# Later loads, a transposed table of probabilities, and a state update moved behind its result, in a gated recurrence followed by an expert layer

## The chip, the cores and the metric

The kernel runs on one core of a Trainium2 chip. The metric is the device time of one execution in microseconds; of several runs, the median is given. A profile is one further execution, taken by the hardware profiler; its durations are used for sums, and its own time stands beside them.

Engines are named as in the profile: PE (TensorE, matmul), PEld (its weight loads), DVE (VectorE), ACT (ScalarE), POOL (GpSimd), SP (SyncE, which here only issues DMAs). A name with a q behind it (SPq) is the engine's instruction queue.

## The reference

Two blocks follow each other. The first is a gated linear recurrence over 768 positions, for 4 batches and 8 heads of 48 numbers:

```python
for t in range(S):
    state = alpha[:, :, t, :, None] * state + np.einsum('bhd,bhe->bhde', k[:, :, t], v[:, :, t])
    y[:, :, t] = np.einsum('bhd,bhde->bhe', q[:, :, t], state)
```

Its result, as rows x of 384 numbers (3072 rows), goes through four experts, weighted by probabilities:

```python
p = domain_probs / (domain_probs.sum(-1, keepdims=True) + 1e-09)
for e in range(E):
    h = np.maximum(x @ w1[e], 0.0)
    out += p[:, e:e + 1] * (h @ w2[e])
```

All inputs and the output are float32.

## The kernel before

**Units and groups.** The recurrence is cut into 24 units of 128 positions of one batch (all 8 heads), numbered 0 to 23 in the order block of positions, then batch. Units come in groups: group 0 has units 0 and 1, groups 1 to 5 have four units each, group 6 has units 22 and 23. For each group and each expert the kernel runs `up` (x @ w1, L710) for eight slices of the 1024 hidden columns, then `down` (h @ w2, L773). From group 1 on, both are computed from operands split into a top part and a rest in float32r, three products each: L745 is the `up` matmul (128x512, nine per slice), L814 the `down` matmul (128x384).

**Order.** The program's order on every engine is the order in which Python emits it. The attention of a unit is a generator with 17 steps (0 to 16, L432 to L703). `deal()` (L860) gives every step of units 2 to 23 a due time from assumed costs of `up` and `down`; `advance()` (L908) runs the steps that are due between two matmuls of `down` or two slices of `up`. Steps of one unit thus lie among the expert matmuls of an earlier group and among steps of the next unit. Units 11 to 17 tie two due times to the unit ahead (`TOGETHER`): their step 7 falls together with step 15 of the unit ahead, their step 11 with its step 16.

**One unit, late kind.** Units 10 to 19 are called `moved` in the code (L611). Step 0 turns the gates on DVE (L444) and lets SP load the next unit's gates into the same buffer (`sa`). Steps 1 and 2 do so for keys (`sk`, `rk`) and queries (`sq`, `rq`, and L170, L171). Steps 3 to 10 build scaled keys and queries. Step 11 computes the far and last near scores on PE (L602, L536) and turns the scaled keys on DVE (L614). Step 12 stores these turned keys to a DRAM buffer `over` (L623), step 13 loads them back into AT in another arrangement, in four DMAs (L630). Step 14 does nothing for these units. Step 15, `result()`, has 56 matmuls into `yps` (L652), copied to xT. Step 16 has 32 small matmuls of AT and the values rv into `sps` (L683), two multiply-and-add pairs on DVE that bring the state `st` up to date (L699, L700), and the load of the values of unit u + 2 into the same buffer rv (L702, issued at L165). Other units compute `sps` at L689 from an AT that PE has turned.

**The start.** Unit 0 has its own code, `first_unit` (L249), written out by hand, with steps of unit 1 in between (`next(other)`). It scores into two tiles, `diag` and `later_half`, which lie in the float32r weight buffers of later use. `take(li)` copies masked scores into `diag` by DVE; for level 0 these are the odd columns. On SP the order is: inputs of units 0 and 1; four pieces of w1 of expert 0 (`raw`, L202, 384 KB each); from L368 the inputs of unit 2 (14 DMAs, behind three POOL memsets); the probabilities (L944, 24 x 128 rows of 16 bytes); four pieces of w2 (L206); then the rest. After `first_unit` a hand-written list (L947) places the remaining steps of units 0 and 1 among the first `up` and `down`. `norm_probs` (L233) divides the probabilities by their sums, in four DVE operations after half of the first `up`.

**Weights.** SP loads raw weights once; ACT and DVE split them, POOL stores the split pieces to DRAM (`kept`), and SP loads them again for each later group (L195, 768 KB a piece). A load into a weight buffer waits for the matmuls that read the piece before it. SP issues in order, so a DMA that waits holds all behind it.

**Places.** Pools lie one behind the other in each partition: `const`, `wts` (w1, w2), `work` (first `dot`, 64 bytes, then raw, AT, QT, KT, xT), `hid` (`room`, 96 bytes that nothing uses, then hT and acc).

Of the kernel before, what the change touches and what calls it, by code (L numbers as in the profile page):

```python
# [10 lines left out]
F32 = mybir.dt.float32  # L11
# [5 lines left out]
AX = mybir.AxisListType  # L17
# [3 lines left out]
def kernel(  # L21
# [11 lines left out]
    nc = tc.nc  # L33

    B, H, S, D = q.shape
    E, DM, F = moe_w1.shape
    P = 128
    NCB = S // P
    NP = H // 2
    HD = 64  # L40
    QUAD = 32
    VD = D + QUAD
    KC = DM // P
    FCH = F // P
    NT = B * P
    NQ = 4
# [7 lines left out]
    n = np.arange(QUAD)[None, :]  # L54
# [8 lines left out]
    const = ctx.enter_context(tc.tile_pool(name="const", bufs=1))  # L63
    wts = ctx.enter_context(tc.tile_pool(name="wts", bufs=2))
    dram = ctx.enter_context(tc.tile_pool(name="dram", bufs=1, space=bass.MemoryType.DRAM))
    work = ctx.enter_context(tc.tile_pool(name="work", bufs=2))
# [4 lines left out]
    ident = ident_all[:, :P]  # L71
# [2 lines left out]
    NBLK = B * NCB  # L74
    p_all = const.tile([P, NBLK, E], F32, name="p_all")
    tot = const.tile([P, NBLK], F32, name="tot")

    near = const.tile([P, H, HALF], F32, name="near")
    lat = const.tile([P, H, P], F32, name="lat")
# [21 lines left out]
    rows_of = {nm: const.tile([P, n, H, D], F32, name=f"r{nm}") for nm, n in (("k", 1), ("q", 2), ("a", 1))}  # L101
    early = {nm: runs_of[nm].rearrange("p a n -> p (a n)")[:, :H * HD].rearrange("p (h d) -> p h d", d=HD)
             for nm in "akq"}
    work.tile([P, 2, H], F32, name="dot", bufs=1)
    hid.tile([P, 24], F32, name="room", bufs=1)
    spare = hid.tile([P, 4, NT], F32, name="hT", bufs=NQ)
    apart = {nm: spare[:, i].rearrange("p (h d) -> p h d", d=HD) for i, nm in enumerate("akq")}
    values = [const.tile([P, H, VD], F32, name=f"rv{i}") for i in range(2)]
# [34 lines left out]
    fresh = lambda gi: gi == 1  # L143


    def load(u, names):
        if u >= len(units):
            return
        cb, b = units[u]
        for nm in names:  # L150
            src = srcs[nm][b, :, cb * P:(cb + 1) * P, :].rearrange("h s d -> s h d")
            if u == by_pairs and nm == "q":
                nc.gpsimd.memset(rows_of["a"], 1.0)
            if u == in_runs and nm != "v":
                nc.gpsimd.memset(runs_of[nm][:, :, RUN - HD // 4:], 0.0)
            for g in range(P // QUAD if u >= in_runs and nm != "v" else 0):
                i, tail = divmod(g, 2)
                off, n = (QUAD, RUN - HD // 4) if tail else (0, RUN)
                runs = srcs[nm][b].rearrange("(a i) s d -> i a (s d)", i=2)[
                    i, :, cb * P * D:(cb + 1) * P * D].rearrange("a (t n) -> t a n", t=QUAD)  # L160
                nc.sync.dma_start(out=runs_of[nm][QUAD * g:QUAD * (g + 1), :, :n],
                                  in_=runs[:, :, off:off + n])
            if u >= in_runs and nm == "a":
                continue
            nc.sync.dma_start(out=raw(u, nm)[:, :, :D], in_=src)  # L165
            if u >= by_pairs and nm == "q":
                odd = srcs["q"][b].rearrange("h (t two) d -> two t h d", two=2)[1, cb * HALF:(cb + 1) * HALF]
                decay = srcs["a"][b].rearrange("h (t two) d -> two t h d", two=2)[1, cb * HALF:(cb + 1) * HALF]
                for first in range(2):
                    nc.sync.dma_start(out=rows_of["q"][first::2, 1], in_=odd)  # L170
                nc.sync.dma_start(out=rows_of["a"][::2, 0], in_=decay)  # L171
# [13 lines left out]
    SPLIT_AT = {1: 2, 4: 3}  # L185
    BESIDE = [{1: 0, 2: 1, 3: 2, 4: 3}, {1: 2, 2: 3}]

    def load_piece(l, i, beside=False):
        if i >= E * NQ * LAST:
            return  # L190
        gi, k = divmod(i, E * NQ)
        e, c = divmod(k, NQ)
        if gi > l:
            w = wt[l][i] = parts_of(l)
            nc.sync.dma_start(out=w.bitcast(F32), in_=kept[l][k])  # L195
            return
        if l == 1 and gi == 0 and not beside:
            return
        w = work.tile([P, KC * QF], F32, name="raw", bufs=RAW)
        wt[l][i] = w  # L200
        if l == 0:
            nc.sync.dma_start(  # L202
                out=w.rearrange("p (c f) -> p c f", f=QF),
                in_=moe_w1[e].rearrange("(c p) f -> p c f", p=P)[:, :, c * QF:(c + 1) * QF])
        else:
            nc.sync.dma_start(  # L206
                out=w.rearrange("p (c d) -> p c d", d=DM),
                in_=moe_w2[e].rearrange("(c p) d -> p c d", p=P)[:, c * FPQ:(c + 1) * FPQ])
# [22 lines left out]
            next(splitting[-1])  # L231

    def norm_probs():  # L233
        nc.vector.reduce_sum(out=tot, in_=p_all, axis=AX.X)
        nc.vector.tensor_scalar_add(out=tot, in0=tot, scalar1=1e-9)
        nc.vector.reciprocal(out=tot, in_=tot)
        nc.vector.tensor_mul(p_all, p_all, tot.unsqueeze(2).broadcast_to([P, NBLK, E]))


    def halves(t, m):  # L240
# [8 lines left out]
    def first_unit(fill, other):  # L249
# [29 lines left out]
        def same_q(li):  # L279
            old, new = (used(t, li) for t in QTs[li:li + 2])  # L280
            nc.scalar.copy(out=new[:, :, :, 0, :], in_=old[:, :, :, 0, :])
# [30 lines left out]
        def take(li, outs):  # L312
            for i in range(2):
                to = diag[:, NP * i:NP * (i + 1)]
                if li < 0:
                    nc.vector.copy_predicated(
                        to, masks_all[:, 6 * QUAD:].unsqueeze(1).broadcast_to([P, NP, HALF]), outs[i])
                    continue
                m = LEVELS[li]
                mk = masks[:, li, :].rearrange("p (b r) -> p b r", r=m)  # L320
                nc.vector.copy_predicated(
                    to.rearrange("p a (b two r) -> p a b two r", two=2, r=m)[:, :, :, 1, :],
                    mk.unsqueeze(1).broadcast_to([P, NP, QUAD // m, m]),
                    outs[i].rearrange("p a (b r) -> p a b r", r=m))
# [40 lines left out]
        same_q(4)  # L365
        next_k(3)
        same_k(3)
        load(2, "akq")  # L368
        products(3, part(second, QUAD))
        take(0, part(first, 0))  # L370
        same_q(5)
        next_q(5)
        scored(part(second, HALF, HALF), KTs[0], lambda p, i, s: plain[rows[i], p, keys[s]])
# [22 lines left out]
        for half, copy in ((0, nc.vector.tensor_copy), (1, nc.scalar.copy)):  # L396
            of = slice(NP * half, NP * (half + 1))
            copy(out=later_half[HALF:, of], in_=diag[HALF:, of])
        fill(1)
        next(other)  # L400

# [30 lines left out]
    def attention(u):  # L432
# [26 lines left out]
            turn("k", KT)  # L459
        else:  # L460
            nc.scalar.copy(out=KT, in_=turned(pair(rk)))
        dot = work.tile([P, 2, H], F32, name="dot", bufs=1)

        def pair_terms():
            both = rows_of["q"]
# [203 lines left out]
                nc.scalar.copy(out=AT, in_=turned(lambda p: KT[:, p, :]))  # L669


        for step in (turn_keys, result) if u >= half else (result, turn_keys):
            step()
            yield

        if cb < NCB - 1:
            KB = AT
            apart_ = u + 1 in in_pairs or moved
            sps = ps.tile([P, NP, 1 if apart_ else 2, D], F32, name="sps", tag="w")
            for p in range(NP if moved else 0):  # L680
                for g in range(P // QUAD):
                    at = QUAD * (NP * g + p)
                    nc.tensor.matmul(sps[QUAD * g:QUAD * (g + 1), p, 0],  # L683
                                     lhsT=KB.rearrange("x a n -> x (a n)")[:, at:at + QUAD],
                                     rhs=rv[:, 2 * p + g // 2, :D], start=True, stop=True)
            for p in range(0 if moved else NP):
                for i in range(2) if apart_ else [slice(0, 2)]:
                    rows = slice(HD * i, HD * (i + 1)) if apart_ else slice(0, P)
                    nc.tensor.matmul(  # L689
                        sps[rows, p], lhsT=KB[:, p, rows],  # L690
                        rhs=rv[:, 2 * p + i, :D] if apart_ else rv[:, 2 * p:2 * p + 2, :D],
                        start=True, stop=True)
            for i in range(2):
                rows = slice(HD * i, HD * (i + 1))
                old, add = st[rows, :, i, :], sps[rows, :, 0 if apart_ else i, :]
                if cb == 0:
                    nc.vector.tensor_copy(out=old, in_=add)
                else:
                    nc.vector.tensor_mul(old, old, decs[-1][rows].broadcast_to([HD, NP, D]))  # L699
                    nc.vector.tensor_add(old, old, add)  # L700
# [213 lines left out]
    with tc.manual_schedule():  # L914
# [11 lines left out]

        load(0, "aqkv")
        load(1, "akqv")
        for i in range(NQ):
            load_piece(0, i)  # L930


# [4 lines left out]
        def fill(times, n=P):  # L937
            for _ in range(times):
                nc.tensor.matmul(idle[:, :n], lhsT=zeros[:, :P], rhs=zeros[:, :n], start=True, stop=True)
# [1 line left out]
        runs = [None, attention(1)]  # L941
        fill(7)
        runs[0] = first_unit(fill, runs[1])
        nc.sync.dma_start(out=p_all, in_=moe_domain_probs.rearrange("(n p) e -> p n e", p=P))  # L944

        span = cost(0, 0, 0) * FCH / 2 + cost(1, 0, 0)
        waiting.extend((span * (k + 1) / 15, u, runs[u])  # L947
                       for k, u in enumerate([1, 1, 1, 0, 1, 0, *[1] * 8]))
        for fc in range(FCH):
            up(0, 0, fc, slice(0, 1))  # L950
            if fc == FCH // 2:
                norm_probs()
            advance(cost(0, 0, 0) / 2)
        down(0, 0, [0])
        while waiting:
# [44 lines left out]
```

## Time and profile before

| what | us |
|---|---|
| median of 3 runs | 1001.29 (999.69 to 1004.07) |
| the profiled execution | 1002.28 |
| its span, first to last instruction | 1000.5 |
| PE busy / DVE busy / ACT busy / POOL busy | 976.8 / 580.6 / 402.5 / 51.4 |
| L814 matmuls on `w`, x2112 | 380.7 |
| L745 matmuls on `w`, x1440 | 336.4 |
| DVE's L700 idle for `sps` of L683 | 22.0 in 9 |

Busy time of PE is that of matmuls in flight, whose ends are modelled. The mean granted clock of PE is 0.996 of full speed; it stands at 0.5 in two stretches of 3.41 us, from 16.62 and from 122.43 us, and at full speed from 6.38 us on otherwise, up to the last microsecond. In the chain that ended last, L814 has 38% of the span and L745 33%. DMA moved 210 MB, a mean of 210 GB/s.

A row of the timeline gives start, duration, engine, line, operation, out<-in, shapes and count, and in brackets how long the engine was idle before it and what ended that. A row of the waits gives who waited for whom: us in total, times, longest.

### The profile page before, as it was taken

How to read it: one execution, taken by the hardware profiler on the slowest of the kernel's cores; microseconds unless marked ns; L12 is line 12 of the kernel's file. 1: busy time of each engine (PE TensorE's matmuls, PEld its weight loads, DVE VectorE, ACT ScalarE, POOL GpSimd, SP SyncE). 2: the span in 40 equal slices, each digit the busy share in tenths (PEclk: the TensorE clock that was granted, in tenths of full speed). 3: DMA queues.
4: the chain of work that ended last, by engine and by line, in shares of the span. 5: the costliest groups of instructions: out<-in, count | busy, mean ns of one | idle time of the engine just before them, and what ended most of it. 6: DMA issues, size and time to landing. Idle time of an engine off the chain costs nothing.

```text
span 1000.5 us, 20763 instructions
## 1 busy us (share of the span) xinstructions
PE 976.8 (98%) x8388; PEld 866.4 (87%) x8388; DVE 580.6 (58%) x1198; ACT 402.5 (40%) x876; POOL 51.4 (5%) x94
## 2 busy tenths in 40 slices
PE   8899899999999999999999999999999999999998
PEld 7777677988989889889899899898898999999997
DVE  4788868476776656666755746766576521222222
ACT  4767655464452542523533413445334422111111
POOL 2000001000101000000000000000000000000000
PEclk9999999999999999999999999999999999999999
DMA  9898979685966885967967769868767406060511
GB/s 191 258 293 220 307 242 351 201 267 170 331 197 204 271 263 147 289 201 216 266 209 243 234 213 264 263 168 283 246 180 246 158 1 221 32 224 30 224 44 32
DMA packets 189999, 210.21 MB, mean 210 GB/s; under 512 B 111408, under 2 KB 165040, under 8 KB 189904
## 3 DMA queue, kind: packets, MB, share of 16 engines
q1 hardware_dynamic: 183440, 179.04, 59.0%
q0 software_dynamic: 6016, 29.49, 7.6%
q8 instruction: 66, 1.08, 0.4%
q10 hardware_dynamic: 448, 0.36, 0.1%
q14 instruction: 29, 0.24, 0.1%
HBM read 176.34 MB, written 32.51 MB: 209 GB/s over the span
## 4 chain that ended last, share of the span: by engine, by line
PE 83%; DVE 7%; ACT 5%; issue 2%; DMA 1%; SPq 1%; DVEq 0%; POOL 0%; ACTq 0%; POOLq 0%
PE ops L814 38%; PE one L745 33%; PE sc L536 4%; PE yps L652 3%; ACT qb L508 2%; PE far L602 1%; DVE near L546 1%; DVE w L220 1%; PE one L739 1%; DVE QT L515 1%; DVE hT L770 1%; PE tp L246 1%; DVE KT L529 1%; ACT KT L528 1%; DVE QT L444 1%
## 5 line engine op out<-in xcount | busy, mean ns | idle before, releaser
L814 PE MATMUL ops<-w,hT 128*128 128x384 f32 x2112 | 380.7, 338 | 1.0 <-DVE hT L770 1.0
L814 PEld LDWEIGHTS ops<-w,hT 128*128 128x128 f32 x2112 | 364.2, 188 | 6.1 <-DVE hT L770 2.5
L745 PE MATMUL one<-xT,w 128*128 128x512 f32 x1440 | 336.4, 393 | 0.0
L745 PEld LDWEIGHTS one<-xT,w 128*128 128x128 f32 x1440 | 269.3, 188 | 58.3 <-DVE hT L770 0.5
L747 ACT ACTIVATE hT<-one 128x512 fp32r<-128x512 f32 (+1 forms) x192 | 108.0, 563 | 310.2 <-PE one L745 308.5
L770 DVE SCALAR_TENSOR_TENSOR hT<-one,hT 128x512 fp32r<-128x512 f32 (+1 forms) x192 | 121.6, 642 | 106.7 <-ACT hT L747 106.6
L508 ACT COPY qb<-QT 64x256 f32<-64x256 f32 x294 | 119.7, 407 | 77.6 <-DVE QT L515 62.2
L515 DVE TENSOR_TENSOR QT<-QT,AT 128x256 f32<-128x256 f32 x158 | 68.2, 431 | 79.9 <-ACT qb L508 78.6
L840 DVE SCALAR_TENSOR_TENSOR acc<-ops,p_all,acc 128x384 f32<-128x384 f32 x66 | 38.1, 612 | 89.1 <-PE ops L814 89.1
L546 DVE COPY_PREDICATED near<-masks,sc 128x256 f32<-128x256 uint8 x124 | 63.5, 512 | 16.3 <-PE sc L536 14.2
L536 PEld LDWEIGHTS sc<-qb,KT 128*64 128x64 f32 x1984 | 63.3, 138 | 9.7 <-issue 4.4
L536 PE MATMUL sc<-qb,KT 128*64 128x64 f32 x1984 | 67.9, 223 | 3.6 <-ACT qb L508 3.6
L529 DVE TENSOR_TENSOR KT<-KT,AT 128x256 f32<-128x256 f32 x161 | 68.0, 423 | 0.8 <-PE tp L246 0.8
L528 ACT COPY KT<-KT 128x256 f32<-128x256 f32 x124 | 51.5, 415 | 5.0 <-DVE KT L529 2.1
L739 PE MATMUL one<-xT,raw 128*128 128x256 f32 (+1 forms) x240 | 45.1, 340 | 0.4 <-ACT xT L416 0.4
L814 PE MATMUL ops<-raw,hT 128*128 128x384 f32 x128 | 44.7, 493 | 0.0
L517 DVE TENSOR_TENSOR AT<-AT 128x256 f32<-128x256 f32 (+1 forms) x138 | 41.5, 301 | 4.7
L458 ACT ACTIVATE AT<-AT,ident 128x512 f32<-128x512 f32 x22 | 15.9, 724 | 66.5 <-PE ops L814 45.2
L739 PEld LDWEIGHTS one<-xT,raw 128*128 128x128 f32 x240 | 38.1, 191 | 5.2 <-ACT xT L416 0.6
L652 PE MATMUL yps<-lat,rv 128*32 128x128 f32 x736 | 34.4, 279 | 2.6 <-ACT lat L627 2.6
L814 PEld LDWEIGHTS ops<-raw,hT 128*128 128x128 f32 x128 | 23.2, 190 | 13.9 <-issue 0.8
L745 PE MATMUL one<-raw,w 128*128 128x256 f32 x288 | 34.6, 279 | 0.0
(118 smaller groups left out, 630.7 us busy)
## 6 DMA issues: line engine op xcount, KB each, us to landing
w<-kept SPq DMA_DIRECT2D x144, 768.0 KB, 6.6
kept<-w POOLq DMA_DIRECT2D x32, 768.0 KB, 7.1
raw<-in_moe_w_dram SPq DMA_DIRECT2D x48, 384.0 KB, 7.3
rv<-in_v_dram SPq DMA_DIRECT2D x24, 192.0 KB, 3.2
rk<-in_k_dram SPq DMA_DIRECT2D x22, 192.0 KB, 3.4
rq<-in_q_dram SPq DMA_DIRECT2D x22, 192.0 KB, 7.2
out_dram<-acc POOLq DMA_DIRECT2D x22, 192.0 KB, 3.1
sa<-in_alpha_dram SPq DMA_DIRECT2D x44, 88.0 KB, 2.3
```

The lines of the kernel that those rows point to most:

```text
L508: nc.scalar.copy(out=qb[rows, :, i, :].rearrange("p a (b r) -> p a b r", r=m), in_=qv[rows])
L515: nc.vector.tensor_mul(qv, qv, spread(dv[:, :, :, 0], m))
L528: nc.scalar.copy(out=new[:, :, :, 1, :], in_=old[:, :, :, 1, :])
L529: nc.vector.tensor_mul(new[:, :, :, 0, :], old[:, :, :, 0, :], spread(halved(decs[li])[:, :, :, 1], m))
L536: nc.tensor.matmul(out[HALF * s:HALF * (s + 1), 2 * p:2 * p + 2, :], lhsT=KTs[li][:, p, HALF * s:HALF * (s + 1)], rhs=qbs[li][:, p, :, QUA ...
L546: nc.vector.copy_predicated(near.rearrange("p a (b two r) -> p a b two r", two=2, r=m)[:, :, :, 1, :], mk.unsqueeze(1).broadcast_to([P, H, ...
L652: nc.tensor.matmul(yps[QUAD * j:QUAD * (j + 1), c, :], lhsT=lhsT, rhs=rhs, start=begins, stop=ends)
L739: nc.tensor.matmul(one, lhsT=w[:, kc], rhs=xTs[gi][:, 0, kc, lo:hi], start=(kc == 0), stop=(kc == KC - 1))
L745: nc.tensor.matmul(one, lhsT=w[:, of_w, kc], rhs=x_part(gi, of_x)[:, kc, :n], start=k == 0, stop=k == len(turns) - 1)
L747: nc.scalar.activation(out=parts[0], in_=one, func=ACT.Relu)
L770: nc.vector.scalar_tensor_tensor(out=low, in0=x, scalar=0.0, in1=top.bitcast(F32), op0=ALU.max, op1=ALU.subtract)
L814: nc.tensor.matmul(sums[slot], lhsT=h, rhs=w, start=(n == begins[slot]), stop=(n == ends[slot]))
```

## The change

There are five edits.

1. Of the four first pieces of `raw`, the main program asks for two. The other two are asked for in `first_unit`, after take(0); a POOL copy of one column of `diag` into the first of them stands ahead of its DMA.
2. The inputs of unit 2 (`load(2, "akq")`) are asked for at the end of the work on `later_half`, behind a POOL copy of one column of it into `room`.
3. The probabilities are loaded as 24 rows of 128 x 4 numbers (`p_rows`, new, 2048 bytes in `const`), turned by four PE transposes into PSUM, and normalized from there. `norm_probs` becomes a generator that runs in the list of steps, at place 9.5. In the same list the second remaining step of unit 0 (its `sps` at L425, state copy and load of values) goes from place 5 to 10.5.
4. `dot` moves from the pool `work` to `hid`, ahead of `room`. With that, raw, AT, QT, KT and xT lie 64 bytes lower against w1 and w2, and hT lies against w1 and w2 as before.
5. The `sps` matmuls become a function `key_values()`. For the moved units it is called right behind `result()`, in step 15; for the others it stays in step 16. The DVE update and the load of values stay in step 16.

```diff
+    p_rows = const.tile([NBLK, P, E], F32, name="p_rows")
...
-    work.tile([P, 2, H], F32, name="dot", bufs=1)
-    hid.tile([P, 24], F32, name="room", bufs=1)
+    hid.tile([P, 2, H], F32, name="dot", bufs=1)
+    room = hid.tile([P, 24], F32, name="room", bufs=1)
...
-    def load(u, names):
+    def load(u, names, behind=None):
...
+        if behind is not None:
+            nc.gpsimd.tensor_copy(out=room[:, :1], in_=behind)
...
-    def load_piece(l, i, beside=False):
+    def load_piece(l, i, beside=False, behind=None):
...
         wt[l][i] = w
+        if behind is not None:
+            nc.gpsimd.tensor_copy(out=w[:, :1], in_=behind)
...
     def norm_probs():
-        nc.vector.reduce_sum(out=tot, in_=p_all, axis=AX.X)
+        tp = ps.tile([P, E, NBLK], F32, name="tp", tag="w")
+        for e in range(E):
+            nc.tensor.transpose(tp[:, e, :], p_rows[:, :, e], ident[:NBLK, :NBLK])
+        probs = tp.rearrange("p e n -> p n e")
+        nc.vector.reduce_sum(out=tot, in_=probs, axis=AX.X)
         nc.vector.tensor_scalar_add(out=tot, in0=tot, scalar1=1e-9)
         nc.vector.reciprocal(out=tot, in_=tot)
-        nc.vector.tensor_mul(p_all, p_all, tot.unsqueeze(2).broadcast_to([P, NBLK, E]))
+        nc.vector.tensor_mul(p_all, probs, tot.unsqueeze(2).broadcast_to([P, NBLK, E]))
+        yield
...
-        load(2, "akq")
         products(3, part(second, QUAD))
         take(0, part(first, 0))
+        for i in range(NQ // 2, NQ):
+            load_piece(0, i, behind=diag[:, 0, :1] if i == NQ // 2 else None)
...
             copy(out=later_half[HALF:, of], in_=diag[HALF:, of])
+        load(2, "akq", behind=later_half[:, 0, :1])
         fill(1)
...
-        for step in (turn_keys, result) if u >= half else (result, turn_keys):
-            step()
-            yield
-
-        if cb < NCB - 1:
-            KB = AT
+        def key_values():
             apart_ = u + 1 in in_pairs or moved
             sps = ps.tile([P, NP, 1 if apart_ else 2, D], F32, name="sps", tag="w")
...
+            return sps, apart_
+
+        for step in (turn_keys, result) if u >= half else (result, turn_keys):
+            step()
+            if step is result and moved:
+                new = key_values()
+            yield
+
+        if cb < NCB - 1:
+            sps, apart_ = new if moved else key_values()
...
-        for i in range(NQ):
+        for i in range(NQ // 2):
             load_piece(0, i)
...
-        nc.sync.dma_start(out=p_all, in_=moe_domain_probs.rearrange("(n p) e -> p n e", p=P))
+        nc.sync.dma_start(out=p_rows, in_=moe_domain_probs.rearrange("(n p) e -> n p e", p=P))
...
-        waiting.extend((span * (k + 1) / 15, u, runs[u])
-                       for k, u in enumerate([1, 1, 1, 0, 1, 0, *[1] * 8]))
+        runs.append(norm_probs())
+        waiting.extend((span * (k + 1) / 15, u, runs[u]) for k, u in (
+            *((k, 1) for k in range(3)), (3, 0), (4, 1), *((k, 1) for k in range(6, 10)),
+            (9.5, 2), (10, 1), (10.5, 0), *((k, 1) for k in range(11, 14))))
         for fc in range(FCH):
             up(0, 0, fc, slice(0, 1))
-            if fc == FCH // 2:
-                norm_probs()
             advance(cost(0, 0, 0) / 2)
```

More of the change, by code (lines that the diff above doesn't have):

```diff
@@ L461, in attention @@
             nc.scalar.copy(out=KT, in_=turned(pair(rk)))
-        dot = work.tile([P, 2, H], F32, name="dot", bufs=1)
+        dot = hid.tile([P, 2, H], F32, name="dot", bufs=1)
         def pair_terms():
@@ L683, in attention @@
                     nc.tensor.matmul(sps[QUAD * g:QUAD * (g + 1), p, 0],
-                                     lhsT=KB.rearrange("x a n -> x (a n)")[:, at:at + QUAD],
+                                     lhsT=AT.rearrange("x a n -> x (a n)")[:, at:at + QUAD],
                                      rhs=rv[:, 2 * p + g // 2, :D], start=True, stop=True)
@@ L689, in attention @@
                     nc.tensor.matmul(
-                        sps[rows, p], lhsT=KB[:, p, rows],
+                        sps[rows, p], lhsT=AT[:, p, rows],
                         rhs=rv[:, 2 * p + i, :D] if apart_ else rv[:, 2 * p:2 * p + 2, :D],
                         start=True, stop=True)
+            return sps, apart_
[6 more added lines that the diff above has]
+            sps, apart_ = new if moved else key_values()
             for i in range(2):
```

## The prediction

> **What bounds the kernel now.** I read the page first, then the waits of TensorE, then the waits of SP's DMA queue, then the timeline of one late unit on PE and on SP. The page:
>
> ```profile
> span 1000.5 us, 20763 instructions
> ...
> PE 976.8 (98%) x8388; PEld 866.4 (87%) x8388; DVE 580.6 (58%) x1198; ACT 402.5 (40%) x876; POOL 51.4 (5%) x94
> ...
> PE 83%; DVE 7%; ACT 5%; issue 2%; DMA 1%; SPq 1%; DVEq 0%; POOL 0%; ACTq 0%; POOLq 0%
> ```
>
> PE is busy 98% of the span and holds 83% of the chain that ended last. After 140 us the matmul stream has almost no gaps, so whatever makes PE wait there lengthens the run one for one. The waits of PE (total us, times, longest):
>
> ```profile
> PE sc L305 <- issue: 2.2, 1, 2.2
> PE sps L683 <- DMA AT<-over: 1.8, 1, 1.8
> PE sps L425 <- ACT AT L421: 1.3, 1, 1.3
> ```
>
> The state matmuls (`sps`, L683) of the ten moved units wait for their DMA only once, for 1.8 us, and that wait is what the change touches most. One of these units (unit 13) on PE, then on SP:
>
> ```profile
> 456.05 0.40 PE L652 MATMUL yps<-lat,rv 128*32 128x128 f32 x8
> 456.38 1.62 PE L536 MATMUL sc<-qb,KT 128*64 128x64 f32 x48
> 457.93 12.07 PE L814 MATMUL ops<-w,hT 128*128 128x384 f32 x68
> 469.93 0.55 PE L683 MATMUL sps<-rv,AT 128*32 128x48 f32 x32
> ```
>
> ```profile
> 455.81 0.64 SPq L171 DMA_DIRECT2D ra<-in_alpha_dram  x1
> 456.55 2.82 SPq L630 DMA_DIRECT2D AT<-over  x4
> ```
>
> The last `yps` matmul ends at 456.45. The four AT loads are only issued from 456.55 to 459.4, and the last lands at 460.67 by its semaphore. Today that is hidden: 13.5 us of `sc` and `ops` matmuls stand between `yps` and `sps`.
>
> **State update behind the result.** The change issues the 32 `sps` matmuls straight after `yps` for units 10 to 19, in the same step. PE takes its matmuls in order; queued behind the first `sps` are the next unit's `sc` (48 records) and the 68 `ops` matmuls, and everything waits for them. The AT loads stay in the step two before, and SP's order around them is the same. So PE now waits from the end of `yps` to the last AT landing. From the trace, unit by unit (end of `yps`, last landing, difference): u10 348.31, 351.50, 3.2; u11 378.94, 380.39, 1.5; u12 417.70, 421.57, 3.9; u13 456.45, 460.67, 4.2; u14 495.22, 500.30, 5.1; u15 533.97, 537.97, 4.0; u16 572.74, 577.93, 5.2; u17 611.49, 606.41, none; u18 657.43, 662.25, 4.8; u19 689.81, 696.27, 6.5, of which 1.8 is waited already, so 4.7. Sum 36.6 us. From landing to the first `sps` record the two tight units took 0.16 and 0.36 us; nine times 0.2 makes 1.8. **Together +38.4 us.**
>
> Does AT come earlier in the changed kernel? SP stood a long time behind `sps`, because load(u+2,"v") overwrites the values that `sps` reads:
>
> ```profile
> SPq L165 <- PE sps L683: 67.7, 10, 12.2
> SPq L161 <- DVE AT L444: 63.3, 15, 8.1
> ```
>
> That first wait goes. But the next DMA in SP's order is `sa`, and it waits for the DVE transpose L444 of the next unit (rv issued at 431.78, sa at 436.28), which hangs on PE's `far` and `sc` matmuls just before. From there SP is busy without a gap of its own: sa, sk, rk, five weight pieces of 768 KB, sq, rq, the two L170, ra, then AT at 456.55, with DMA completions as the only waits. That is 24.4 us from sa to the last landing against 20.2 us of PE work to the end of `yps`. Both ends hang on the same place in PE's stream, so an earlier delay does not make the next unit's wait shorter. The DVE wait that goes (L700 behind `sps`, 22.0 us in 9) buys little: PE waits for DVE's `hT` 1.0 us in the whole run. I take 0, bounds -1.0 to 0.
>
> **The clock behind these waits.** Windows of busy time by stretch (length, PE busy and count, PEld, DVE, ACT, POOL, PEclk, DMA share, GB/s):
>
> ```profile
> 13.21:16.62 3.41, 0.95 (x22) 0.64 (x25) 2.27 (x9) 0.41 (x1) 0.00 (x0) 1.00 1.12 302
> 16.62:20.03 3.41, 3.41 (x70) 3.35 (x70) 1.18 (x5) 0.81 (x3) 0.00 (x0) 0.50 0.55 116
> 33.69:37.10 3.41, 1.72 (x12) 0.84 (x13) 2.45 (x9) 2.02 (x5) 0.00 (x0) 1.00 1.04 344
> 119.02:122.43 3.41, 1.59 (x48) 1.31 (x42) 2.33 (x6) 3.20 (x8) 0.05 (x1) 1.00 1.01 320
> 122.43:125.85 3.42, 3.42 (x65) 2.71 (x60) 2.54 (x6) 0.00 (x0) 0.53 (x1) 0.50 1.01 298
> ```
>
> Twice a 3.41 us stretch with PE busy 0.95 and 1.59 us was followed by one at half clock; 1.72 us (and everything fuller) was not. So I take it that over 1.7 us of idle in one such stretch halves the next. A wait of 4.2 us at a random phase gives: the stretch after its first part at half in 1 case of 2, costing 0.9 us of what PE still does there; the stretch after its second part at half in 3 of 4, costing 1.7. That is about 1.6 us a wait. Eight waits are long enough (u11's is not): **+13 us**, bounds 0 and 8 x 3.4 = 27.
> The Trainium skill (TensorE: Matmul & The Clock Gate, the section on why this matters for your kernels) says it differently: one whole idle window, a gap of over about 3 us, sends the clock to half. Read strictly, a whole window must be idle, while this trace halved the clock after windows that were 28% and 47% busy; by the strict reading the term would be the rival's below.
>
> **The first unit.** PE stands 2.2 us at 14.3 with "issue" as the reason. In the DMA packets a 16 KB instruction packet for PE goes out at 14.18 to 15.21, and PE goes on at 16.54. It was due when PE had some 200 instructions behind it (10.1 us); pieces 0 to 2 of `raw`, 72 packets of 50 ns on each DMA engine from 10.5 us, give 14.1. Were pieces 2 and 3 held back, it would go out 1.2 us sooner, and the half-clock stretch from 16.62 would go too: -1.2 - 1.7 = -2.9. But the POOL copy that shall hold them reads column 0 of `diag`, and take(0) writes odd columns only. The program waits by elements touched, not by tile: L281 (ACT) and L286 (DVE) write even and odd columns of one tile and both start at 7.55. So the copy only follows the POOL memset L263 (done 7.27), before SP reaches piece 2 at 9.64. I take 0, bounds -2.9 to 0.
>
> load(2) is really held, until DVE's L398 is done at 20.0 (now from 10.77). Its 14 DMAs at 0.47 us take SP to 27.0; behind them stand the probabilities and the four w2 pieces, 24.04 now, about 27.4 then. They land 6 us after issue (median to 40 us): 33.5 for the first. PE wants it near 32 (L814 now at 32.77); it then has 1.7 us of idle before `far` (36.66, on ACT's `qb`), which covers it. Unit 2's rows are wanted at 47.9. 0, bounds 0 to +1.7. POOL's two copies and three memsets delay nothing: its next work is at 40.71.
>
> Probabilities: 3072 packets of 16 bytes (24.5 to 26.6) become 24 rows; four small transposes on PE (four big ones take 0.66) and four DVE operations (0.98 together) move to before `far`, where PE has the idle time above and DVE stands 2.05 us before L546 at 38.30. ACT wants the result at 43.54. 0.
> Unit 0's state step goes from the fifth place to behind `far`: PE's 1.3 us wait for ACT goes, but its 1.1 us of matmuls then lie after `far`, on the path to `yps` at 40.55. Net 0, bounds -1.3 to +1.1.
>
> **x at 0 towards w1.** Without `dot` in its pool, xT and raw stand 64 bytes lower against w1; hT and w2 keep their distance. The only rows: starts of L745's matmuls are 226, 229 or 232 ns apart, always by the same third of K; other pairings at other distances are other shapes. All 1440 at 226 or at 232: 4.3 us less or more. Far bounds: 216 (L739's widest form) -18.7, and 238 (its slowest stretch, at 288 us) +12. I take 0.
>
> **The sum.** The profiled execution took 1002.28 us (span 1000.5 and 1.8 around it). 1002.3 + 38.4 + 13 = 1053.7. It lies 1.0 above the median of the runs, 1001.29; against that, **1053 us**.
>
> **Rivals.**
> - The waits come, the clock holds better. A wait of S covers a whole 3.41 us stretch with chance (S - 3.41)/3.41: 3.3 stretches over all waits, 5.6 us, so 1045; with none at half, 1040. For: only two dips in the trace. Against: those two followed half-busy stretches. Chance 0.16.
> - **Not slower.** SP, free of its 67.7 us behind `sps`, brings AT in before `yps` ends. It decides from 6.5 us earlier (all waits gone): no 38.4, no 13, and u19's old 1.8 gone: 999.5. Against: the chain from `sa` above. 0.09, with 0.05 more for half-way cases (1010 to 1035).
> - The new place of x is worth the far bound: 1053 - 18.7 = 1034. 0.06.
> - The first pieces are held after all: 1050, inside the forecast.
> The forecast itself (1047 to 1061) 0.60, above it 0.04.
>
> The range 1033 to 1061 takes in the forecast, the clock rival and the place of x; 0.18 is left out. Within 0.5% (what a measurement here can tell from no change) 0.05, faster by more 0.04, slower 0.91.
>
> **What would show it.** Right: `PE sps <- DMA AT` near 40 us in 9 or 10 times; clock rows at 0.50 after several of them; DVE's L700 and SP's L165 no longer behind `sps`; `raw` pieces 2 and 3 still issued near 10 us and the "issue" wait at 14 us still there; L745's starts still 229 apart. Wrong: AT loads issued before `yps` begins, PE's wait below 10 us, or L745 at another spacing.

## The result, and the profile after

The changed kernel takes **1051.28 us** (median of 6 runs, 1048.66 to 1056.3); the kernel before, run beside it, took 1001.51 (6 runs, 999.69 to 1004.07). The ratio is 1.0502, interval 1.0471 to 1.0532: slower by 5%. The profiled execution took 1050.83 us, span 1049.0.

Lines of the changed file are 3 to 17 higher: the moved `sps` is L690 (was L683), the AT loads L642 (L630), `yps` L664 (L652), `sc` L548 (L536), `up` L762 (L745), `down` L831 (L814), SP's loads L164 and L168 (L161 and L165). The page of the kernel after:

```profile
span 1049.0 us, 20763 instructions
...
PE 987.3 (94%) x8392; PEld 879.1 (84%) x8392; DVE 578.5 (55%) x1198; ACT 401.7 (38%) x876; POOL 51.5 (5%) x96
...
PE 74%; DMA 8%; DVE 8%; ACT 4%; SPq 3%; issue 3%; DVEq 0%; POOL 0%; ACTq 0%; POOLq 0%
```

PE's busy time rose by 10.5 us although PE does almost the same work (four small transposes more), which is what a lower clock looks like; the other 38 us of the longer span are idle time. In the chain that ended last, DMA went from 1% to 8% and SPq from 1% to 3%. The waits of PE name the place:

```profile
PE sps L690 <- DMA AT<-over: 39.7, 9, 7.3
...
PE ops L831 <- DMA raw<-in_moe_w_dram: 3.6, 1, 3.6
...
PE sc L315 <- issue: 1.4, 1, 1.4
```

The first line was 1.8 us in 1 wait before. Unit 13 again, the unit shown in the prediction; on PE, then on SP:

```profile
468.08 0.40 PE L664 MATMUL yps<-lat,rv 128*32 128x128 f32 x8
472.60 0.55 PE L690 MATMUL sps<-rv,AT 128*32 128x48 f32 x32 [4.12 <-DMA AT<-over]
473.08 2.83 PE L548 MATMUL sc<-qb,KT 128*64 128x64 f32 x48
475.84 11.45 PE L831 MATMUL ops<-w,hT 128*128 128x384 f32 x63
```

```profile
448.43 2.08 SPq L164 DMA_DIRECT2D sa<-in_alpha_dram  x4
...
467.63 1.04 SPq L174 DMA_DIRECT2D ra<-in_alpha_dram  x1
468.78 1.99 SPq L642 DMA_DIRECT2D AT<-over  x4
```

`sps` now comes ahead of `sc` and `ops`, and PE stands 4.12 us until AT is there. The 48 `sc` matmuls behind the wait take 2.83 us instead of 1.62: the granted clock is 0.50 from 473.00 to 476.42 us.

Where in the run the time went, by the start of each unit's first `yps` matmul (after minus before): +1.3 us at units 1 to 4, -0.2 at unit 5 (a half-clock stretch at 122.43 us is gone), -0.4 at unit 10; then, from unit 11 on, +3.5, 6.2, 12.0, 17.5, 23.9, 29.4, 36.9, 36.4, 41.5 and 48.5 at unit 20, where it stays. The loss is made between 347 and 771 us, behind the moved units. Unit 17 alone, whose AT landed in time, costs nothing: unit 18 is no later than unit 17.

One profile (the first run of the place of x) was taken at a clock of 0.851 throughout and is not read below.

### The profile page after: what moved, and what is told of

It reads as the page before. It is cut to its first block, busy times and chain, and to the rows that moved or that the text cites. A ratio compares the mean times of both kernels' runs of the same rounds, so it can differ in the third digit from the quotient of the medians.

```text
span 1049.0 us, 20763 instructions
## 1 busy us (share of the span) xinstructions
PE 987.3 (94%) x8392; PEld 879.1 (84%) x8392; DVE 578.5 (55%) x1198; ACT 401.7 (38%) x876; POOL 51.5 (5%) x96
## 4 chain that ended last, share of the span: by engine, by line
PE 74%; DMA 8%; DVE 8%; ACT 4%; SPq 3%; issue 3%; DVEq 0%; POOL 0%; ACTq 0%; POOLq 0%
PE ops L831 37%; PE one L762 26%; PE sc L548 5%; DMA w<-kept 3%; PE yps L664 2%; DMA AT<-over 2%; DVE w L225 1%; ACT qb L520 1%; DMA over<-KT 1%; SPq L642 1%; PE far L614 1%; DVE hT L787 1%; PE one L756 1%; DVE near L558 1%; SPq L164 1%
## 5 line engine op out<-in xcount | busy, mean ns | idle before, releaser
L831 PE MATMUL ops<-w,hT 128*128 128x384 f32 x2112 | 382.8, 340 | 1.2 <-DVE hT L787 1.1
L831 PEld LDWEIGHTS ops<-w,hT 128*128 128x128 f32 x2112 | 367.3, 190 | 6.0 <-DVE hT L787 2.6
L762 PE MATMUL one<-xT,w 128*128 128x512 f32 x1440 | 334.1, 391 | 0.0
L762 PEld LDWEIGHTS one<-xT,w 128*128 128x128 f32 x1440 | 269.2, 188 | 56.3 <-DVE hT L787 0.7
L548 PE MATMUL sc<-qb,KT 128*64 128x64 f32 x1984 | 76.0, 238 | 3.6 <-ACT qb L520 3.6
L548 PEld LDWEIGHTS sc<-qb,KT 128*64 128x64 f32 x1984 | 71.1, 152 | 9.0 <-ACT qb L520 4.1
L831 PE MATMUL ops<-raw,hT 128*128 128x384 f32 x128 | 46.3, 505 | 3.6 <-DMA raw<-in_moe_w_dram 3.6
L690 PE MATMUL sps<-rv,AT 128*32 128x48 f32 x320 | 7.1, 246 | 39.7 <-DMA AT<-over 39.7
L690 PEld LDWEIGHTS sps<-rv,AT 128*32 128x32 f32 x320 | 5.8, 136 | 41.9 <-issue 27.6
L831 PEld LDWEIGHTS ops<-raw,hT 128*128 128x128 f32 x128 | 23.9, 196 | 17.7 <-DMA raw<-in_moe_w_dram 3.7
```

The costliest lines, as they stand in the source:

```text
L548: nc.tensor.matmul(out[HALF * s:HALF * (s + 1), 2 * p:2 * p + 2, :], lhsT=KTs[li][:, p, HALF * s:HALF * (s + 1)], rhs=qbs[li][:, p, :, QUA ...
L762: nc.tensor.matmul(one, lhsT=w[:, of_w, kc], rhs=x_part(gi, of_x)[:, kc, :n], start=k == 0, stop=k == len(turns) - 1)
L831: nc.tensor.matmul(sums[slot], lhsT=h, rhs=w, start=(n == begins[slot]), stop=(n == ends[slot]))
```

## The experiments

The theory is the prediction's: PE waits for AT, which SP issues too late, and the waits halve the clock. The rivals are a loss from one of the other four edits, waits without a cost of the clock, and a lateness that no placing of the loads could mend (DMA engines without room).

**1. Everything but the state update.** `sps` goes back to step 16; all else is as in the changed kernel.

```diff
-            if step is result and moved:
-                new = key_values()
...
-            sps, apart_ = new if moved else key_values()
+            sps, apart_ = key_values()
```

> The changed kernel with the sps matmuls of the moved units back in step 16, all else changed. If the whole loss is PE's wait for AT and the clock behind it: PE's wait for AT back to about 2 us in one place, no half-clock windows after 300 us, and a time of 1000 to 1003, that is 48 to 51 less than the changed kernel. If a part of the loss comes from another edit (the late w2 pieces, the new place of x): a time that stays 5 or more above the kernel before.

Measured: 999.29 us (12 runs, 996.93 to 1004.53), ratio to before 0.998 (0.9964 to 0.9996). Of the 50 us nothing is left; the other four edits together gain about 2 us. No stretch after 21 us is at half clock, up to the last microseconds.

```profile
PE sps L690 <- DMA AT<-over: 0.9, 2, 0.7
```

**2. The state update alone,** put into the kernel before (the same edit the other way round, with `key_values()` as in the diff of the change).

> The kernel before with the sps matmuls alone moved behind yps. If this edit carries the loss: 1048 to 1054, PE's wait for AT 38 to 41 us in nine or ten places. If the edits only cost that much together (AT late because of the other moves): under 1030.

Measured: 1053.09 us (4 runs, 1051.58 to 1056.64), ratio 1.0521 (1.0496 to 1.0547).

```profile
PE sps L678 <- DMA AT<-over: 40.7, 9, 8.0
```

The move is enough for the whole loss. The two runs together settle which edit it is. They don't yet tell why AT is late, nor how much of the loss is wait and how much is clock.

**3. The store and the loads of the state on another queue.** The changed kernel, with `over` stored and AT loaded by POOL.

```diff
-            nc.sync.dma_start(out=over, in_=by_quad.rearrange("x t a c -> x t (a c)"))
+            nc.gpsimd.dma_start(out=over, in_=by_quad.rearrange("x t a c -> x t (a c)"))
...
-            nc.sync.dma_start(out=AT[QUAD * t:QUAD * (t + 1)],
+            nc.gpsimd.dma_start(out=AT[QUAD * t:QUAD * (t + 1)],
```

> The changed kernel, with the store to over and the four AT loads issued by POOL in place of SP. If AT is late because SP issues in order and has sa, weights, sq, rq ahead of it: AT is there before yps ends in units 11 to 16, the wait falls from 39.7 us to under 12 (what is left in units 10, 18 and 19) and the time to 1002 to 1018. If AT is late because the DMA engines have no room (the rival): the loads land as late as now, the wait stays over 30 us and the time over 1038.

Measured: 1006.34 us (5 runs, 1005.53 to 1010.35), ratio 1.0059 (1.0035 to 1.0083). The wait, POOL's queue for unit 12, and PE behind it:

```profile
PE sps L690 <- DMA AT<-over: 8.1, 2, 4.8
```

```profile
394.73 0.60 POOL L635 DMA_DIRECT2D over<-KT  x1 [16.19 <-DVE KT L626]
397.92 2.17 POOL L642 DMA_DIRECT2D AT<-over  x4 [2.59 <-PE ops L831]
```

```profile
415.09 0.40 PE L664 MATMUL yps<-lat,rv 128*32 128x128 f32 x8
415.31 0.52 PE L690 MATMUL sps<-rv,AT 128*32 128x48 f32 x32
415.76 1.62 PE L548 MATMUL sc<-qb,KT 128*64 128x64 f32 x48
```

POOL stores `over` as soon as DVE has turned the keys and issues the loads 3.2 us later. The last one lands at 403.15, 12 us before `yps` ends (415.49); the `sps` matmuls follow `yps` without a gap. In the changed kernel DVE has turned unit 12's keys at 402.83, also 21 us before `yps` ends (423.89), but SP stores `over` at 409.15, behind sa, sk, rk and two weight pieces, and issues the loads at 423.45, behind three more weight pieces, sq, rq and ra:

```profile
402.12 0.71 DVE L626 STREAM_TRANSPOSE KT<-KT 128x512 f32<-128x512 f32 x1
```

```profile
403.84 1.76 SPq L164 DMA_DIRECT2D sa<-in_alpha_dram  x4
...
409.15 0.43 SPq L635 DMA_DIRECT2D over<-KT  x1
...
422.64 0.71 SPq L174 DMA_DIRECT2D ra<-in_alpha_dram  x1
423.45 3.18 SPq L642 DMA_DIRECT2D AT<-over  x4
```

So the data was there in time, and the lateness was SP's. Two units still wait, 18 (4.85 us) and 19 (3.2), each with a stretch at half clock behind it (658.78 and 696.33 us): their `over` is stored only 10 and 12 us before their `yps` ends, where the other eight have 17 to 22.

**4. The wait filled.** The changed kernel, with 7 to 20 matmuls that the result does not need (128x192, into `sps` ahead of the real ones) in the nine units that wait.

```diff
+    FILLED = {10: 7, 11: 7, 12: 12, 13: 11, 14: 14, 15: 11, 16: 13, 18: 11, 19: 20}
...
+            for _ in range(FILLED.get(u, 0)):
+                nc.tensor.matmul(sps.rearrange("p a i d -> p (a i d)"), lhsT=lat[:, 0, :],
+                                 rhs=flat_v[:, :NP * D], start=True, stop=True)
```

> The changed kernel, with 7 to 20 extra matmuls (128x192, results overwritten) ahead of sps in each unit that waits, about as long as the wait. If idle time itself halves the clock: no half-clock window in these places, PE's wait for AT under 6 us, time 1039 to 1044, that is 8 to 11 less than the changed kernel. If the clock has nothing to do with the loss: the same time as the changed kernel, 1049 to 1054.

Measured: 1040.31 us (4 runs, 1037.82 to 1041.48), ratio 1.0385 (1.0362 to 1.0409): 11.0 us less than the changed kernel, with 106 matmuls more (212 in the records). The time from the end of `yps` to the first real `sps` is the same, 41 us over nine units against 39.5. The mean clock of this kernel, then that of the changed one:

```profile
core 0: 1036.0 us, clock 0.998
```

```profile
core 0: 1049.0 us, clock 0.979
```

No stretch between 36 us and the last microsecond is at half here. The traces agree with the medians: from unit 10 to unit 20 the delay against the kernel before grows by 37.9 us here and by 48.9 in the changed kernel. So about 11 us of the loss are the clock, shown by giving PE something to do, and the rest is the wait itself.

**5. The place of x alone.** The kernel before, with `dot` in the other pool and nothing else changed; run twice, for the reason given above.

```diff
-    work.tile([P, 2, H], F32, name="dot", bufs=1)
+    hid.tile([P, 2, H], F32, name="dot", bufs=1)
...
-        dot = work.tile([P, 2, H], F32, name="dot", bufs=1)
+        dot = hid.tile([P, 2, H], F32, name="dot", bufs=1)
```

> The kernel before with dot alone moved to the other pool (x at 0 towards w1). If the place matters as the two traces suggest: starts of the 512-wide up matmuls 227 ns apart in the median in place of 229, those of the 256-wide ones of the last two groups 120 in place of 118, together 1 to 3 us less over 1440 and 288 matmuls: 998 to 1000. If the traces differ by chance: 229 and 118, and the time of the kernel before.

> Before, with only the place of x in its row moved by 64 bytes; all else as before. If the place sets the spacing of PE, the 512-wide multiplications with the stationary xT start 227 ns apart instead of 229 and the 256-wide ones 120 instead of 118; 1440 of the first at -1.8 and 288 of the second at +2 give -2.6 + 0.6 = -2 us: 999 to 999.8, ratio about 0.998. If the 2 ns of the other kernels come from something else in the change, the spacing stays at 229 and 118 and the time within 0.5 us of before's.

Measured: 1001.95 us (ratio 0.9985, interval 0.9966 to 1.0003) and 1000.59 (12 runs, 997.64 to 1003.13; ratio 0.9995, 0.9981 to 1.001). The time alone does not tell it from nothing. The trace of the second run does: the starts of the 512-wide `up` matmuls are 227 ns apart in the median instead of 229 (mean of those below 400 ns 228.4 instead of 229.9), those of the 256-wide ones 120 instead of 118. The groups of this kernel:

```profile
L745 PE MATMUL one<-xT,w 128*128 128x512 f32 x1440 | 334.0, 391 | 0.0
L745 PE MATMUL one<-raw,w 128*128 128x256 f32 x288 | 35.2, 283 | 0.0
```

Before, the first had 336.4 busy with a mean of 393. From unit 10 to unit 18 each unit comes 0.145 us sooner than before, 1.2 us in all. By the starts it is 1440 x -1.5 ns = -2.2 us and 288 x 2.2 = +0.6: **about -1.5 us**.

**6. The first pieces really held,** with the state update back in step 16. The POOL copy reads column 1 of `diag`, which take(0) writes, instead of column 0.

```diff
-            load_piece(0, i, behind=diag[:, 0, :1] if i == NQ // 2 else None)
+            load_piece(0, i, behind=diag[:, 0, 1:2] if i == NQ // 2 else None)
```

> The first experiment's kernel (state update in step 16), with the POOL copy ahead of piece 2 reading column 1 of diag, which take(0) writes, in place of column 0. If the program waits by elements and the late instruction packet is what PE stands for at 14 us: pieces 2 and 3 are issued after 11.6 us in place of near 10, the instruction packet goes out about 1 us sooner, the issue wait falls from 2.3 to about 1, and the time by 1 to 3 us against the first experiment (996 to 998). If that wait has another cause: the wait and the time stay.

Measured: 998.21 us, ratio 0.9968 (0.9948 to 0.9988), against 999.29 without the edit; the intervals overlap. Pieces 2 and 3 go out at 12.09 and 12.50 us instead of 9.35 and 9.84 in experiment 1, PE's instruction packet at 13.52 instead of 14.26, and PE stands for "issue" a little less:

```profile
PE sc L315 <- issue: 1.5, 1, 1.5
```

It was 2.3 us in experiment 1. The stretch at half clock behind it stayed (16.08). In the profile, unit 1's `yps` comes 0.9 us sooner. That the held pieces did this is not shown: in the changed kernel, where they are not held, the packet went out at 13.46 us, and PE stood for "issue" only 1.4 us.

**7. Unit 2's inputs asked for behind w2,** on top of 6: `load(2, "akq")` after the four w2 pieces, with no POOL copy ahead of it.

> The kernel of pieces really held, with the inputs of unit 2 asked for behind the four w2 pieces. If the late w2 pieces cost PE 1 to 3.6 us at the first down: that wait (ops on raw for DMA) is gone and the time falls by 1 to 2 us against the pieces held alone. If it lies beside PE's later wait for unit 1's scores: the wait goes and the time stays within 0.7 us.

Measured: 1001.96 us, ratio 1.0003 (0.9982 to 1.0024): 3.75 us more than experiment 6, which neither forecast had.

```profile
PE y L425 <- issue: 2.8, 1, 2.8
PE sps L689 <- DMA AT<-over: 2.3, 1, 2.3
...
PE far L613 <- DVE tot L244: 1.9, 1, 1.9
```

The wait for the first w2 piece is gone. But the w2 pieces are now issued (from 13.50 us) ahead of PE's second instruction packet, which goes out at 19.07 instead of 17.1 to 18.5, and PE stands for "issue" 2.8 us there; PE's wait for the probabilities (`tot`) is longer too, 1.9 us against 0.6 in experiment 1. Other waits took the place of the one removed: unit 1's `yps` comes 2.2 us later than in experiment 6. The rest lies at unit 18, where PE waits 2.3 us for AT and a stretch at half clock follows (663.41); that the edit caused this part is not shown.

**8. The move only where AT is in time.** Experiment 3, with the early `sps` for units 10 to 17 only; 18 and 19 keep it in step 16.

```diff
-            if step is result and moved:
+            if step is result and moved and u < in_pairs[-1] + 1:
...
-            sps, apart_ = new if moved else key_values()
+            sps, apart_ = new if moved and u < in_pairs[-1] + 1 else key_values()
```

> The changed kernel with over and AT issued by POOL and the sps matmuls behind yps for units 10 to 17 only; units 18 and 19 in step 16. If the third experiment lost only in units 18 and 19 (8.1 us of wait and two half-clock windows of 1.7): PE's wait for AT under 1.5 us, time 994 to 998, below both kernels. If an early update has a cost of its own (PE, PSUM, POOL): 1000 or more.

Measured: **996.46 us** (9 runs, 994.29 to 999.63), ratio to before 0.9948 (0.993 to 0.9966). It beats both kernels.

```profile
span 996.0 us, 20820 instructions
```

```profile
PE sps L690 <- DMA AT<-over: 2.1, 1, 2.1
```

The one wait left, 2.1 us where under 1.5 was expected, is that of unit 18, whose `sps` stands in step 16. From unit 11 to unit 17 each unit gains 0.27 us on the kernel before, against 0.145 with the place of x alone. The other 0.125 us is what the early `sps` gains when AT is there. In unit 12 its 32 small matmuls cost 0.34 us between `yps` and `sc`, and the 0.48 us that they took between `ops` and `far` in experiment 1 are gone. Eight times 0.125 is 1.0 us: this is all that the traces show for the move. The median lies 2.8 us below that of experiment 1, while the spans of the two profiled executions are equal (996.0 and 995.7); what makes the other 1.8 us is not shown.

**9. Experiments 6 and 8 together.**

> The kernel of the run in which only units 10 to 17 take the state early, with POOL issuing the state's store and loads, and with the POOL copy reading column 1 of the mask, so that the last two pieces of the raw weights really go out later. If the two small terms add, the pieces leave at about 12.1 and 12.5 us, the first instruction packet of PE at about 13.5 us instead of 14.1, and the time is 0 to 1 us below that run's 996.46: about 995.8. If the held pieces only move the wait to the first w2 piece or to the second instruction packet, the time is 996.5 or more, with a new wait in the first 40 us.

Measured: 996.38 us (5 runs, 995.94 to 997.04), ratio 0.995 (0.9934 to 0.9966); 0.1 us from experiment 8. The packet goes out at 13.57 instead of 14.13, yet unit 1's `yps` comes 0.56 us later than in experiment 8. Part of it is a wait that was 0.6 us there:

```profile
PE far L614 <- DVE tot L244: 1.0, 1, 1.0
```

Holding the pieces is worth nothing that these runs can show.

## Why the prediction was right, and where it was off

The forecast, 1053 us, is 1.7 from the 1051.28 measured, and its main steps hold.

- **The wait for AT: +38.4 predicted, +37.9 measured, in part by luck** (39.7, less the 1.8 that stood there before). Unit by unit the forecast was 3.2, 1.5, 3.9, 4.2, 5.1, 4.0, 5.2, none, 4.8, 6.5 us to the landing; the time to the first `sps` was 2.6, 2.8, 4.4, 4.1, 5.2, 4.3, 5.0, none, 4.0, 7.3. Experiments 1 and 2 put it on this edit, 3 on SP's order. The landings in the prediction are read too early, though: each of these DMAs signals sixteen times, and its figures are the third signal of the last load, not the sixteenth. By the sixteenth, the kernel before gives 3.5, 1.7, 4.1, 4.4, 5.3, 6.0, 5.4, none, 4.9, 6.7 (460.89 instead of 460.67 in unit 13, 539.96 instead of 537.97 in unit 15), which is 40.3 without the 1.8 already waited; the first `sps` followed the landing by 0.04 and 0.14 us in the two tight units, not 0.16 and 0.36. The sum would then have been about 41 us, 3 more than came.
- **SP doesn't bring AT sooner.** In unit 13, `sa` to the first AT issue takes 20.35 us (20.27 before) and `sa` to the end of `yps` 20.05 (20.17 before). Of the 67.7 us behind `sps`, 11.9 are left; the rest went, and the wait for the next DVE transpose, which was 63.3, grew by 82. The waits of SP's queue after:

```profile
SPq L164 <- DVE AT L456: 145.3, 16, 19.1
...
SPq L168 <- PE sps L690: 11.9, 9, 2.2
```

- **The clock: +13 predicted, 11 to 12 measured.** Experiment 4 gives 11.0. The sum of the trace gives 12.2: the delay grows by 48.85 us from unit 10 to unit 20, of which 37.9 are waits, and the place of x takes back 1.3. So the rivals with 5.6 us or nothing are out. (The prediction's two parts make 1.7 us a wait rather than 1.6, and 13.8 in all.) The size is right, but **the threshold behind it is not**: it put the limit at 1.7 us of idle time in one stretch of 3.41 us. Windows of the changed kernel (columns as in the prediction):

```profile
12.21:15.62 3.41, 1.80 (x37) 0.97 (x27) 3.07 (x11) 1.30 (x5) 0.00 (x0) 1.00 0.97 327
15.62:19.03 3.41, 3.32 (x69) 3.26 (x69) 1.00 (x5) 0.73 (x2) 0.00 (x0) 0.50 0.09 29
```

```profile
380.85:384.26 3.41, 1.59 (x56) 1.32 (x50) 1.99 (x5) 1.76 (x4) 0.45 (x1) 1.00 0.68 140
384.26:387.67 3.41, 2.48 (x82) 2.38 (x83) 2.18 (x6) 1.09 (x4) 0.54 (x1) 1.00 0.87 290
425.22:428.63 3.41, 0.32 (x29) 0.35 (x32) 0.68 (x3) 1.21 (x3) 0.99 (x1) 1.00 0.48 108
428.63:432.04 3.41, 3.41 (x72) 3.18 (x60) 1.78 (x5) 0.89 (x3) 0.00 (x0) 0.50 0.97 391
```

A stretch with PE busy 1.80 us (half of it two 128x384 matmuls, the rest small ones, 64x64) was followed by half clock; one with 1.59 (`yps`, 128x32 on 128 columns) was not; and in the kernel before, another with 1.59 (`sc`, 128x64 on 64 columns) was. Busy time as the profile counts it is not what the clock goes by; what is, stays open. The strict reading of the Trainium skill (TensorE: Matmul & The Clock Gate, the section on why this matters for your kernels), that a whole idle window is needed, does not hold either: of the eight times that the clock fell between 300 us and the last microseconds, four followed a wholly idle stretch and four one that was busy 0.3 to 1.2 us.
The estimate took the phase as random, and it was not. From 428.63 to 606.12 us the clock fell every 44.37 us, which is 13 stretches of 3.413: units 12 to 16 of the changed kernel are 44.3 to 45.1 us apart, so each of these waits fell on the stretches in much the same way. That the estimate came out near is in part luck.
- **The first pieces are not held: right.** They go out at 9.80 and 10.28 us, as they did. The bound for the other case, -2.9, was too wide: experiment 6 gave -0.9 in the profile and 9 gave nothing, and the half-clock stretch did not go with the shorter wait.
- **load(2) and w2: 0 predicted, mis-sized.** PE waited 3.58 us for the first w2 piece, which landed at 33.2, as the working said (33.5). PE wanted it at 29.65 rather than 32, and there is a half-clock stretch from 32.69 on top. Together with what was gained there, unit 1's `yps` came 1.3 us later, inside the bound of 1.7. In the other kernels with this order (1, 3, 4, 6, 8 and 9) the wait was 0.8 to 2.1 us, and unit 1's `yps` came 0.2 to 1.6 us sooner than before. The row of the timeline:

```profile
33.23 3.61 PE L831 MATMUL ops<-raw,hT 128*128 128x384 f32 x6 [3.58 <-DMA raw<-in_moe_w_dram]
```

- **x at 0: 0 predicted, -1.5 measured,** inside the near bound of 4.3. The prediction expected a spacing of 229 ns still; it is 227. The far bound of -18.7 is out.
- **Unit 0's state step and the probabilities: 0 predicted, not settled.** The 1.3 us wait for ACT is gone from the list, and in the changed kernel no wait in the first 40 us can be put down to either. But `far` stands behind `tot` for 0.6 us in experiments 1 and 8, 1.0 in 9 and 1.9 in 7, a wait that the kernel before does not have. The two edits were not tried singly.

Why the intended gain did not come: before, matmuls stood between `yps` and `sps`, 13.5 us of them in six of the ten units (11.9 in unit 17, 4 to 5 in units 10, 18 and 19), and AT could land in that time. The move takes away that cover for a gain of 0.125 us a unit; where AT is really there (experiment 8), the gain is as small as that.

## What to carry to other kernels

Before a consumer is moved forward on an in-order engine, compare the landing of its operands with its new place, instance by instance: here nine subtractions in the trace forecast 38.4 us of waiting (41 with the last signal of each load), and 37.9 came. A transfer that lands late may only have been issued late: here the same loads, issued from a queue without other DMAs ahead of them, landed 12 us before `yps` ended instead of 4 us after it (unit 12). Move the consumer only for the instances in which the data is then there. Count the clock as a term of its own: here, with waits of 2.6 to 7.3 us, it added nearly a third to them.

## What the runs showed of the hardware

- 64 bytes in the place of one operand change the pace of fp32r matmuls by 1 to 2%: 229 to 227 ns at 512 columns, 118 to 120 at 256, in the other direction, in each of the nine traces with x at the new place; the two with x at the old place (the kernel before and experiment 2) have 229 and 118.
- The first 16 KB instruction packet for PE after the start went out between 12.82 and 14.60 us in eleven kernels, and PE, which stood for "issue", went on 2.2 to 2.5 us after it each time. That these packets wait behind queued data is argued from experiment 7 (the second one at 19.07, behind the w2 pieces), not shown.
- The sixteen signals of one DMA can lie far apart: in unit 15 of the kernel before, fifteen of the last AT load's came by 538.22 us and the sixteenth at 539.96.
- The half clock can hold on: in the changed kernel, after half-clock stretches with PE busy 0.67 us (from 735.83) and 2.39 us (from 606.12) the next one was at half too, though PE was busy all through it; after its others, with 2.87 us or more, it was at full speed. Busy time does not decide this either: in experiment 2 a stretch with 2.75 us (from 696.62) was followed by full speed, and in experiment 9 one with 3.20 us by half:

```profile
15.58:18.99 3.41, 3.20 (x68) 3.13 (x68) 0.89 (x4) 0.73 (x2) 0.00 (x0) 0.50 0.08 24
18.99:22.41 3.42, 3.42 (x71) 2.76 (x70) 2.15 (x5) 1.31 (x3) 0.44 (x4) 0.50 0.38 90
```
